# Attention in pieces between the units of a feed-forward layer

## The chip, the cores and the metric

The kernel runs on one core of one Trainium2 chip. The metric is the device time of one execution in microseconds, the median of several runs.

## The reference

Three stages follow one another. First attention over 4 batches, 8 heads, 576 positions and head size 64, with masks: heads 0 to 3 see the last 32 positions, heads 4 to 7 the earlier positions with the same remainder by 32.

```
scores = q @ k.T / 8, masked; attn = softmax(scores); x = attn @ v
x = x as (2304 tokens, 512)
h = max(x @ w1_in, 0);  x = (h * h) @ w1_out            # 512 -> 2048 -> 512
h = x @ w2_in
g = (a0 + a1 h + a2 h^2 + a3 h^3) / (1 + |b0||h| + |b1|h^2 + 1e-6)
out = g @ w2_out                                        # 512 -> 2048 -> 512
```

The weights come as 64-bit floats, the rest as 32-bit.

## The kernel before

The 2304 tokens are cut into six blocks of 384 (j = 0 to 5), the 2048 inner features into 16 slices of 128 (f = 0 to 15). Layer 1 runs all (j, f) in order, then layer 2 does. One step (j, f) of layer 1 is an h unit (`h_unit`, L412: 12 matmuls over four slices of the input, with each operand split into a high and a low part, three products), its activation (`act1`), and the output unit of the step two before (`o_unit1`, L452: 12 matmuls into four accumulators). Layer 2 has the same shape (L412, L605).

Attention is cut into 48 groups of two heads of one batch: a local group covers 192 queries, a strided one 14 or (every third pair of the strided) 4 of the 32 remainders. Groups are loaded and scored in pairs. A group goes through these functions: `at_scores` (a pair at a time, two PSUM banks; L277 puts the mask in by a matmul for groups before 24, L294 adds it on VectorE after that; L285 is q times k), `at_max` (L296, L297), `at_exp` (L309, four exponentials on ScalarE from the scores' bank), `at_norm` (L317, L318, and L320, where GpSimd multiplies e by the reciprocal), `at_transpose` (L327 on TensorE into a bank, L333 or L335 copies it to `at`), `at_values` (L343, a bank), and `at_out` (L368 on ScalarE and L369 on VectorE split the result into the high and low part of the layer's input). `last[j]` is the last group that block j needs: 9, 19, 23, 33, 43, 47.

The order is that of "slots" (`at_slot`). Slot n loads up to group n + 4, scores a pair if n is even, does the maximum of group n, the values of an earlier group, the transposes of one or two, the exponentials and the norm of n. The lags are three slots to the transposes and four to the values for groups before 12, two and three after that. Slots 0 to 13 run before layer 1 begins; the rest are put ahead of the h units by the table `ends`, always two slots at a time:

```
while slot < min(want, goal) or slot % 2 and slot < ends[-1]:
    at_slot(slot)
    slot += 1
```

By this two slots stand before units (0,0), (0,3), (0,6), (0,10), (0,13), (1,2), (1,6), (1,10), (2,0), (2,3), (2,7), (2,11), (3,0), (3,3), (3,6), (3,10), (3,13) and (4,3), a last one before (4,11).

PSUM has a pool of seven banks (tag "ps") for scores, transposes, values, h and accumulators, and one more bank (`psum_w`). An even block's four accumulators are all in the pool; an odd block's first one lies in the bank aside:

```
acc[j] = [acc_bank(f"acc0_{j}_{e}", e == 0 and j % 2 == 1) for e in range(KT)]
```

Weights of layer 1 are loaded raw (L189), turned into 32-bit floats with bit operations (`to_f32`: L201 on ScalarE, L202 to L204 on VectorE) and split (`split_w`: L218, L220, L221). The first four of 32 pieces are done in slots 10 to 13, the rest in block 0, two a step. In block 0 the low parts of the activation (L430) are VectorE's too. In blocks 1 to 4 the weights of layer 2 are converted in the same way and stored in memory (`spill_w`), eight pieces a block. Three blocks of the layer's input can live at a time.

All loads and stores are issued from SP's queue, in its order. q and k of a pair are one load (L250), its values another (L253); past group 12 each has two buffers. At the start SP issues q and k of the first pair, the masks, the first values, the identity, the coefficients `a` and `b` (L476, L477, broadcast to all partitions), and then q, k and values of three further pairs. ScalarE's first instruction is the absolute value of `b` (L478).

The program gives instructions in this order; a planner then orders each engine's queue by that order and by its own estimate of when operands and buffers are ready, except where `keep_in_program_order` or `issue_after` bind it (groups before 12 on TensorE, and layer 2). On the chip each engine follows its queue in order and waits where the real time comes later.

Of the kernel before, what the change touches and what calls it, by code (L numbers as in the profile page):

```python
# [9 lines left out]
F32 = mybir.dt.float32  # L10
# [3 lines left out]
AF = mybir.ActivationFunctionType  # L14
# [4 lines left out]
P = 128  # L19
B, H, S, D = 4, 8, 576, 64  # L20
# [5 lines left out]
NB = NT // TB  # L26
NF = DFF // P
# [98 lines left out]
QK_W = 1008  # L126
# [30 lines left out]
def moe_kernel(ctx, tc, qk, vp, w1, w2, a, b, masks, eye, out):  # L157
    nc = tc.nc
    groups = _groups()
    last = _last_group(groups)  # L160
    NG = len(groups)
# [70 lines left out]
    st = {}  # L232
    loaded = [0]
    FIRST, PLACES, LATE, WARM = 12, 8, 24, 10

    def lags(n):

        return (3, 4) if n < FIRST else (2, 3)

    def at_load(n):  # L240

        g, p = groups[n], n // 2
        if n < FIRST:
            t = wpool.tile([P, QK_W], F32, tag=f"wh{NF - 1 - p}", name=f"qk{g.name}")
            vt = wpool.tile([P, 2, 2, 2, D], F32, tag=f"w{'hl'[p % 2]}{7 - p // 2}", name=f"v{g.name}")
        else:
            t = apool.tile([P, QK_W], F32, tag="qk", name=f"qk{g.name}")
            vt = apool.tile([P, 2, 2, 2, D], F32, tag="v", name=f"v{g.name}")
        w = 2 * (g.qn + g.kn)
        nc.sync.dma_start(t[:, :w], qk[p][:, :w])  # L250
        if n == 0:
            nc.sync.dma_start(cst, masks)
        nc.sync.dma_start(vt, vp[p].rearrange("p (m t h d) -> p m t h d", m=2, h=2, d=D))  # L253
        for m in range(2):
            st[n + m] = dict(qk=t[m * D : (m + 1) * D], v=vt[:, m])

    def at_scores(n):

# [55 lines left out]
    def at_norm(n):  # L314
        g, s = groups[n], st[n]
        sm, nn = s["sm"], s["nn"]
        nc.gpsimd.tensor_scalar(sm[: g.nq, 8 : 8 + nn], sm[: g.nq, 8 : 8 + nn], 1.0, 1e-9, ALU.mult, ALU.add)  # L317
        nc.vector.reciprocal(sm[: g.nq, 12 : 12 + nn], sm[: g.nq, 8 : 8 + nn])  # L318
        r = sm[: g.nq, 12 : 12 + nn, None].to_broadcast([g.nq, nn, g.nk])
        nc.gpsimd.tensor_tensor(s["e"], s["e"], r, ALU.mult)  # L320
# [50 lines left out]
    def pin(n, ins):  # L371
        if n < FIRST:
            tc.keep_in_program_order(ins)

    def load_groups(n):
        while loaded[0] < min(NG, n):
            at_load(loaded[0])
            loaded[0] += 2

    def at_slot(n):  # L380

        load_groups(n + 4)
        if n < NG and n % 2 == 0:
            at_scores(n)
        if n < NG:
            at_max(n)
        if n == 2:
            warm_up(2)
        for m in range(max(0, n - 4), min(n, NG)):
            if n - m == lags(m)[1]:  # L390
                at_values(m)
        for m in range(max(0, n - 4), min(n, NG)):
            if n - m == lags(m)[0]:
                at_transpose(m)
        if n < NG:
            at_exp(n)
        for m in range(max(0, n - 4), min(n, NG)):
            if n - m == lags(m)[1]:
                at_out(m)
        if n < NG:  # L400
            at_norm(n)


    gt, acc, lows = {}, {}, []
# [66 lines left out]
            tc.keep_in_program_order(nc.tensor.matmul(wps, warm[:, :P], warm, start=True, stop=True))  # L471

    warm_up(6)
    load_groups(1)
    nc.sync.dma_start(ident, eye)
    nc.sync.dma_start(co[:, 0:4], a[None, :].to_broadcast([P, 4]))  # L476
    nc.sync.dma_start(co[:, 4:6], b[None, :].to_broadcast([P, 2]))  # L477
    nc.scalar.activation(co[:, 6:8], co[:, 4:6], AF.Abs)  # L478


    LAG, LATER = 2, 3
# [22 lines left out]
    def feed_w(n):  # L504
        for _ in range(n):
            load_raw(fed[0])
            if fed[0] < len(wq):
                f, part = wq[fed[0]]
                c = slice(part * DM, (part + 1) * DM)
                wh, wl = wt[0, f] if part else w_place(0, f)  # L510
                split_w(wh[:, c], wl[:, c], to_f32(0, f, part, raws[fed[0]]))
                fed[0] += 1

    load_groups(8)
    slot = 0
    while slot < last[0] + lags(0)[1] + 1:
        at_slot(slot)
        slot += 1
        load_raw(fed[0])
        if slot > 9:  # L520
            feed_w(1)
    steps = [(j, f) for j in range(NB) for f in range(NF)]
    prev = []

    attn_open = True
    n2 = 0

    def spill_w(f, part):
# [98 lines left out]

    prev2 = []
    LAG2, EARLY = 6, 5
    ends = [slot, 23, 30, 38, 47, 51]  # L630
    spills = (0, 8, 16, 24, 2 * NF)
    for j, f in steps:
        if attn_open:
            goal, start_slot = ends[j + 1], ends[j]
            want = start_slot + -(-(goal - start_slot) * (f + 1) // (NF - 1))
            while slot < min(want, goal) or slot % 2 and slot < ends[-1]:
                at_slot(slot)
                slot += 1
            if slot >= ends[-1]:
                attn_open = False  # L640
        while lows:
            lows.pop()()
        if j == 0:
            feed_w(2)
        ps = psum.tile([P, 512], F32, tag="ps", name=f"h0_{j}_{f}")
        h_unit(0, j, f, ps)
        last_act = act1(j, f, ps)
        if 0 < j < 5 and n2 < spills[j - 1] + -(-(spills[j] - spills[j - 1]) * (f + 1) // NF):
            with tc.issue_after(last_act):
                spill_w(n2 // 2, n2 % 2)  # L650
            n2 += 1
            if n2 == 2 * NF:
# [39 lines left out]
```

## Time and profile before

| what | value |
|---|---|
| time, median of 3 runs (lowest to highest) | 936.13 us (935.17 to 940.32) |
| the profiled execution's own time | 937.38 us |
| its span, first to last instruction | 935.6 us |
| TensorE matmul busy | 900.8 us, 96% |
| VectorE busy | 675.2 us, 72% |
| GpSimd busy | 595.5 us, 64% |
| ScalarE busy | 550.7 us, 59% |
| mean granted TensorE clock | 0.982 |
| first h unit; first h unit of block 5 | 47.84 us; 457.10 us |

Busy times are shares of the whole span, in which the stages have different limits: the time before the first h unit, block 0 with the weights' conversion, blocks 1 to 4 with attention, block 5, and layer 2. Matmuls overlap in the pipeline, so a run of twelve is read from start to start and not as twelve durations. A granted clock of 1.00 is 2.4 GHz, 0.50 is 1.2 GHz, and a figure between the two is the mean over a stretch that had both.

### The profile page before, as it was taken

The page shows a single profiled execution, that of the slowest core. Times are in us where ns is not written, and L with a number is a line of the kernel's source. Part 1 is how long each engine was busy: PE and PEld are TensorE (multiplying, and loading weights), DVE is VectorE, ACT ScalarE, POOL GpSimd, SP SyncE. Part 2 cuts the span into 40 slices and gives each one's busy share as a digit, 9 for nine tenths or more (in the row PEclk, how much of TensorE's full clock was granted, in tenths as well). Part 3 has the DMA queues.
Part 4 walks back from the last instruction along what each step waited for, and adds up shares of the span by engine and source line. Part 5 has one row for each costly group of instructions (what it writes and reads, how often), then busy time and mean ns, then how long its engine had stood idle before and what let it go on. Part 6 is the DMA issues. An engine that isn't in the chain of part 4 may idle for free.

```text
span 935.6 us, 14609 instructions
## 1 busy us (share of the span) xinstructions
PE 900.8 (96%) x5232; PEld 828.8 (89%) x5232; DVE 675.2 (72%) x792; ACT 550.7 (59%) x1391; POOL 595.5 (64%) x643
## 2 busy tenths in 40 slices
PE   6799989999989999999999999999999999999998
PEld 3598789998889898999999999999999899899896
DVE  3897965546444455434412589999999999999997
ACT  5786654445443544433324767777777776777774
POOL 3576755555444445534423478888888888888885
PEclk9799989999999999999999999999999999999999
DMA  8773334435433533433267530010010010100000
GB/s 294 258 268 120 121 111 167 165 112 192 151 121 98 170 101 130 145 124 113 95 234 262 194 133 9 9 50 9 9 51 9 18 43 9 43 1 1 34 1 34
DMA packets 40104, 98.55 MB, mean 105 GB/s; under 512 B 4704, under 2 KB 11616, under 8 KB 40032
## 3 DMA queue, kind: packets, MB, share of 16 engines
q1 hardware_dynamic: 40032, 97.62, 31.2%
q8 instruction: 41, 0.67, 0.3%
q14 instruction: 31, 0.25, 0.1%
HBM read 71.39 MB, written 26.21 MB: 104 GB/s over the span
## 4 chain that ended last, share of the span: by engine, by line
DVE 42%; PE 39%; ACT 2%; POOL 2%; issue 1%; DMA 1%; SPq 0%; POOLq 0%; ACTq 0%
DVE rq L572 23%; PE h L412 19%; PE acc L452 16%; DVE p L574 9%; DVE rq L583 7%; PE ps_t L327 1%; PE ps_v L343 1%; POOL spl L221 1%; PE ps_s L285 1%; DMA x_scratch<-x 1%; DVE r L426 1%; PE acc L605 1%; ACT w L201 1%; DVE w L202 0%; DVE w L203 0%
## 5 line engine op out<-in xcount | busy, mean ns | idle before, releaser
L412 PE MATMUL h<-xh,wh 128*128 128x384 f32 x768 | 260.3, 339 | 2.0 <-ACT at L335 0.9
L412 PE MATMUL h<-xh,wl 128*128 128x384 f32 x768 | 258.9, 337 | 0.0
L412 PE MATMUL h<-xl,wh 128*128 128x384 f32 x768 | 258.6, 337 | 0.0
L572 DVE RECIPROCAL rq<-w 128x384 f32<-128x384 f32 x96 | 243.9, 2541 | 17.2 <-POOL w L570 17.2
L412 PEld LDWEIGHTS h<-xh,wh 128*128 128x128 f32 x768 | 145.4, 189 | 8.7 <-ACT p L569 2.0
L412 PEld LDWEIGHTS h<-xl,wh 128*128 128x128 f32 x768 | 145.3, 189 | 3.8
L412 PEld LDWEIGHTS h<-xh,wl 128*128 128x128 f32 x768 | 145.2, 189 | 0.0
L430 POOL TENSOR_TENSOR gl<-r,gh 128x384 fp32r<-128x384 f32 x75 | 75.8, 1011 | 108.3 <-ACT gh L429 90.9
L591 POOL TENSOR_TENSOR gl<-rq,gh 128x384 fp32r<-128x384 f32 x96 | 115.1, 1199 | 39.8 <-ACT gh L590 39.8
L452 PE MATMUL acc<-gh,wh 128*128 128x384 f32 x384 | 132.2, 344 | 0.0
L452 PE MATMUL acc<-gh,wl 128*128 128x384 f32 x384 | 130.9, 341 | 0.8 <-POOL wl L221 0.8
L426 DVE TENSOR_TENSOR r<-r 128x384 f32<-128x384 f32 x75 | 54.4, 726 | 107.0 <-ACT r L422 106.9
L452 PE MATMUL acc<-gl,wh 128*128 128x384 f32 x384 | 131.3, 342 | 0.0
L570 POOL TENSOR_TENSOR w<-w,sq 128x384 f32<-128x384 f32 x96 | 97.5, 1015 | 46.5 <-ACT sq L567 46.3
L571 POOL TENSOR_TENSOR p<-p,hs 128x384 f32<-128x384 f32 x96 | 114.7, 1194 | 0.0
L605 PE MATMUL acc<-wh,gl 128*128 128x512 f32 x288 | 114.1, 396 | 0.3 <-POOL gl L591 0.3
L605 PE MATMUL acc<-wl,gh 128*128 128x512 f32 x288 | 113.7, 395 | 0.0
L605 PE MATMUL acc<-wh,gh 128*128 128x512 f32 x288 | 112.0, 389 | 0.0
L590 ACT CAST gh<-rq 128x384 fp32r<-128x384 f32 x96 | 49.4, 514 | 106.1 <-DVE rq L583 106.1
L422 ACT ACTIVATE r<-h 128x384 f32<-128x384 f32 x91 | 44.7, 491 | 98.7 <-PE h L412 94.5
L574 DVE SCALAR_TENSOR_TENSOR p<-p,co,hs 128x384 f32<-128x384 f32 x96 | 99.2, 1033 | 0.0
L429 ACT CAST gh<-r 128x384 fp32r<-128x384 f32 x91 | 46.8, 514 | 71.5 <-DVE r L426 71.1
(76 smaller groups left out, 1577.2 us busy)
## 6 DMA issues: line engine op xcount, KB each, us to landing
wraw<-in_w SPq DMA_DIRECT2D x64, 512.0 KB, 4.3
w_scratch<-sph SPq DMA_DIRECT2D x32, 256.0 KB, 4.0
w_scratch<-spl SPq DMA_DIRECT2D x32, 256.0 KB, 3.1
wh<-w_scratch SPq DMA_DIRECT2D x16, 512.0 KB, 3.7
wl<-w_scratch SPq DMA_DIRECT2D x16, 512.0 KB, 4.5
v<-in_vp SPq DMA_DIRECT2D x24, 256.0 KB, 4.7
qk<-in_qk SPq DMA_DIRECT2D x12, 416.0 KB, 4.6
x_scratch<-x SPq DMA_DIRECT2D x24, 192.0 KB, 3.1
```

The costliest lines, as they stand in the source:

```text
L412: nc.tensor.matmul(ps[:, :TB], w[:, c], x[:, kk, :], start=(kk == 0 and i == 0), stop=(kk == KT - 1 and i == 2))
L426: nc.vector.tensor_tensor(h, h, h, ALU.mult)
L430: low = lambda: (nc.vector if psum_h or j == 0 else nc.gpsimd).tensor_tensor(gl, h, gh.bitcast(F32), ALU.subtract)
L452: nc.tensor.matmul(acc[j][e][:, :TB], w[:, c], g, start=(f == 0 and i == 0), stop=(f == NF - 1 and i == 2))
L570: keep(nc.gpsimd.tensor_tensor(w, w, sq, ALU.add))
L571: keep(nc.gpsimd.tensor_tensor(p1, p1, hs, ALU.mult))
L572: keep(nc.vector.reciprocal(rq, w))
L574: keep(nc.vector.scalar_tensor_tensor(p1, p1, a1, hs, ALU.add, ALU.mult))
L583: keep(nc.vector.scalar_tensor_tensor(rq, p1, a0, rq, ALU.add, ALU.mult))
L590: keep(nc.scalar.copy(gh, rq))
L591: keep(nc.gpsimd.tensor_tensor(gl, rq, gh.bitcast(F32), ALU.subtract))
L605: nc.tensor.matmul(p, g[:, t * P : (t + 1) * P], w[:, c], start=(f == 0 and i == 0), stop=(f == NF - 1 and i == 2))
```

## The change

Slots stay for groups up to slot 13. Past them attention is a list of pieces, and at most one stands before a unit. A piece is either the values of group v with the transposes of group v + 1, or a pair's scores with maximum, exponentials and norms of both groups. Two of the first kind come, then one of the second. `paces` spreads the 55 pieces over blocks 0 to 4 as 14, 10, 13, 13 and 5. q and k of the pair after next are loaded after a pair's scores, values of the pair after next after the pair's second values; both from pair 8 on. At the start Exp is ScalarE's first instruction, q and k of the second pair are loaded ahead of the first values, and the coefficients are loaded (and their absolute value taken) before unit (3,0).

```diff
+    def load_qk(p):            # q and k of pair p; load_v(p) likewise its values
...
     def load_groups(n):
-        while loaded[0] < min(NG, n):
-            at_load(loaded[0])
+        while loaded[0] < min(2 * AHEAD_PAIRS, n):      # AHEAD_PAIRS = 8
+            load_qk(loaded[0] // 2)
+            load_v(loaded[0] // 2)
             loaded[0] += 2
+    def pieces(n):
+        t, v = n - 3, n - 4
+        yield from ()
+        while v < NG:
+            for _ in range(2):
+                yield v, t
+                v, t = v + 1, t + 1
+            if n < NG:
+                yield n
+                n += 2
+
+    def at_piece(piece):
+        nonlocal slot
+        if isinstance(piece, int):
+            at_scores(piece)
+            for n in (piece, piece + 1):
+                at_max(n)
+                at_exp(n)
+                at_norm(n)
+            load_qk(piece // 2 + 2)
+            return
+        v, t = piece
+        if v < NG:
+            at_values(v)
+            slot = max(slot, v + 5)
+        if t < NG:
+            at_transpose(t)
+        if v < NG:
+            at_out(v)
+            if v % 2 and v // 2 + 2 >= AHEAD_PAIRS:
+                load_v(v // 2 + 2)
...
     warm_up(6)
-    load_groups(1)
+    nc.scalar.activation(co[:, 9:10], co[:, 8:9], AF.Exp)
+    load_qk(0)
+    nc.sync.dma_start(cst, masks)
+    load_qk(1)
+    load_v(0)
     nc.sync.dma_start(ident, eye)
-    nc.sync.dma_start(co[:, 0:4], a[None, :].to_broadcast([P, 4]))
-    nc.sync.dma_start(co[:, 4:6], b[None, :].to_broadcast([P, 2]))
-    nc.scalar.activation(co[:, 6:8], co[:, 4:6], AF.Abs)
+    load_v(1)
+    loaded[0] = 4
+    def load_co():             # the three lines above, as they were
...
-    ends = [slot, 23, 30, 38, 47, 51]
+    load_qk(AHEAD_PAIRS)
+    todo = list(pieces(slot))
+    due_by = [next(i for i, p in enumerate(todo) if isinstance(p, tuple) and p[0] == last[j]) + 1 for j in range(1, NB)]
+    paces = [due_by[0], max(due_by[1], due_by[0] + 10), max(due_by[2], due_by[0] + 23), due_by[3], len(todo)]
+    done = [0]
     for j, f in steps:
-        if attn_open:
-            goal, start_slot = ends[j + 1], ends[j]
-            want = start_slot + -(-(goal - start_slot) * (f + 1) // (NF - 1))
-            while slot < min(want, goal) or slot % 2 and slot < ends[-1]:
-                at_slot(slot)
-                slot += 1
+        if j < NB - 1:
+            start = paces[j - 1] if j else 0
+            want = start + -(-(paces[j] - start) * (f + 1) // NF)
+            while done[0] < want:
+                at_piece(todo[done[0]])
+                done[0] += 1
...
+        if (j, f) == (3, 0):
+            load_co()
```

## Rows read from the trace of the kernel before

**Rows 1.** The page: busy tenths of TensorE and its granted clock, 40 slices.

```profile
PE   6799989999989999999999999999999999999998
...
PEclk9799989999999999999999999999999999999999
```

**Rows 2.** Stretches from block to block: length, each engine's busy us (instructions), clock, DMA.

```profile
47.84:136.34 88.50, 81.42 (x512) 74.87 (x511) 73.49 (x132) 59.69 (x171) 62.96 (x76) 0.94 0.44 150
136.34:217.31 80.97, 80.97 (x556) 77.29 (x556) 43.24 (x72) 38.93 (x117) 41.52 (x52) 1.00 0.49 159
217.31:307.49 90.18, 84.49 (x537) 79.06 (x537) 42.64 (x81) 39.96 (x130) 41.99 (x56) 0.96 0.41 133
307.49:386.46 78.97, 76.59 (x504) 72.06 (x504) 40.77 (x82) 38.20 (x124) 40.79 (x55) 0.98 0.41 129
386.46:457.10 70.64, 69.60 (x418) 68.11 (x418) 30.98 (x46) 24.24 (x49) 31.38 (x31) 1.00 0.35 115
457.10:519.50 62.40, 62.40 (x362) 62.40 (x362) 13.48 (x19) 23.12 (x48) 20.84 (x22) 1.00 0.65 228
```

**Rows 3.** The same stretches, TensorE's instructions of L452 alone, blocks 0 to 4.

```profile
47.84:136.34 88.50, 36.77 (x168) 0.94 0.44 150
136.34:217.31 80.97, 40.18 (x203) 1.00 0.49 159
217.31:307.49 90.18, 41.55 (x205) 0.96 0.41 133
307.49:386.46 78.97, 34.68 (x171) 0.98 0.41 129
386.46:457.10 70.64, 36.35 (x193) 1.00 0.35 115
```

**Rows 4.** Block 0, TensorE's instructions of L277 alone (mask matmuls).

```profile
47.84:136.34 88.50, 2.08 (x8) 0.94 0.44 150
```

**Rows 5.** Waits of TensorE, 47.8 to 457 us: us in total, times, longest.

```profile
PE ps_t L327 <- ACT e L309: 5.8, 5, 1.7
PE ps_t L327 <- DVE xl L369: 5.1, 3, 2.5
PE ps_v L343 <- ACT at L335: 3.3, 4, 1.0
```

**Rows 6.** Timeline of one burst in block 2: start, us, what [idle before].

```profile
228.15 0.48 PE L285 MATMUL ps_s<-qk 64*72 64x72 f32 x8
...
231.98 0.32 ACT L309 ACTIVATE e<-ps_s,sm 72x72 f32<-72x72 f32 x1 [2.33 <-POOL sm L297]
...
232.06 0.30 DVE L294 TENSOR_TENSOR ps_s<-ps_s,cst 72x144 f32<-72x144 f32 x1
...
232.74 0.65 PE L327 MATMUL ps_t<-ident,e 126*126 126x126 f32 x4 [1.73 <-ACT e L309]
...
235.21 0.30 ACT L309 ACTIVATE e<-ps_s,sm 72x72 f32<-72x72 f32 x1
```

**Rows 7.** VectorE's groups in block 0: count | busy us, mean ns | idle before.

```profile
L204 DVE SCALAR_TENSOR_TENSOR wraw<-wraw,bits 128x512 int32<-128x512 int32 x28 | 19.1, 683 | 0.7
...
L296 DVE TENSOR_REDUCE sm<-ps_s 96x4 f32<-96x512 f32 (+1 forms) x8 | 4.6, 581 | 0.0
```

**Rows 8.** Stretches before the first h unit, columns as in rows 2.

```profile
41.20:47.84 6.64, 6.20 (x58) 4.78 (x56) 5.96 (x13) 6.17 (x29) 3.22 (x8) 0.74 0.69 222
20.50:47.84 27.34, 20.55 (x193) 15.01 (x189) 24.66 (x55) 21.67 (x100) 14.59 (x30) 0.81 0.80 274
```

**Rows 9.** Timeline of the start.

```profile
3.06 0.43 SPq L477 DMA_DIRECT2D co<-in_b  x1
...
7.72 0.20 POOL L297 TENSOR_SCALAR sm<-sm 126x4 f32<-126x4 f32 x1 [7.28 <-DVE sm L296]
...
9.55 0.20 ACT L478 ACTIVATE co<-co 128x2 f32<-128x2 f32 x1 [7.54 <-DMA co<-in_b]
...
10.81 1.67 PE L285 MATMUL ps_s<-qk 64*126 64x126 f32 x16 [3.32 <-DMA qk<-in_qk]
```

More of the change, by code (lines that the diff above doesn't have):

```diff
@@ L238, in lags, with load_v @@
         return (3, 4) if n < FIRST else (2, 3)
-    def at_load(n):
-        g, p = groups[n], n // 2
+    def load_qk(p):
+        n = 2 * p
+        if n >= NG:
+            return
+        g = groups[n]
         if n < FIRST:
             t = wpool.tile([P, QK_W], F32, tag=f"wh{NF - 1 - p}", name=f"qk{g.name}")
+        else:
+            t = apool.tile([P, QK_W], F32, tag="qk", name=f"qk{g.name}")
+        w = 2 * (g.qn + g.kn)
+        nc.sync.dma_start(t[:, :w], qk[p][:, :w])
+        for m in range(2):
+            st[n + m] = dict(qk=t[m * D : (m + 1) * D])
+    def load_v(p):
+        n = 2 * p
+        if n >= NG:
+            return
+        g = groups[n]
+        if n < FIRST:
             vt = wpool.tile([P, 2, 2, 2, D], F32, tag=f"w{'hl'[p % 2]}{7 - p // 2}", name=f"v{g.name}")
         else:
-            t = apool.tile([P, QK_W], F32, tag="qk", name=f"qk{g.name}")
             vt = apool.tile([P, 2, 2, 2, D], F32, tag="v", name=f"v{g.name}")
[L249 to L252, printed above, removed]
         nc.sync.dma_start(vt, vp[p].rearrange("p (m t h d) -> p m t h d", m=2, h=2, d=D))
         for m in range(2):
-            st[n + m] = dict(qk=t[m * D : (m + 1) * D], v=vt[:, m])
+            st[n + m]["v"] = vt[:, m]
     def at_scores(n):
@@ L373, in pin @@
             tc.keep_in_program_order(ins)
+    AHEAD_PAIRS = 8
     def load_groups(n):
-        while loaded[0] < min(NG, n):
-            at_load(loaded[0])
+        while loaded[0] < min(2 * AHEAD_PAIRS, n):
+            load_qk(loaded[0] // 2)
+            load_v(loaded[0] // 2)
             loaded[0] += 2
@@ L382, in at_slot @@
         load_groups(n + 4)
-        if n < NG and n % 2 == 0:
+        if n % 2 == 0:
             at_scores(n)
-        if n < NG:
-            at_max(n)
+        at_max(n)
         if n == 2:
             warm_up(2)
-        for m in range(max(0, n - 4), min(n, NG)):
+        for m in range(max(0, n - 4), n):
             if n - m == lags(m)[1]:
                 at_values(m)
-        for m in range(max(0, n - 4), min(n, NG)):
+        for m in range(max(0, n - 4), n):
             if n - m == lags(m)[0]:
                 at_transpose(m)
-        if n < NG:
-            at_exp(n)
-        for m in range(max(0, n - 4), min(n, NG)):
+        at_exp(n)
+        for m in range(max(0, n - 4), n):
             if n - m == lags(m)[1]:
                 at_out(m)
-        if n < NG:
-            at_norm(n)
+        at_norm(n)
[14 more added lines that the diff above has]
+            for n in (piece, piece + 1):
+                at_max(n)
+                at_exp(n)
+                at_norm(n)
+            load_qk(piece // 2 + 2)
+            return
+        v, t = piece
[8 more added lines that the diff above has]
+                load_v(v // 2 + 2)
     gt, acc, lows = {}, {}, []
@@ L473, in moe_kernel @@
     warm_up(6)
-    load_groups(1)
-    nc.sync.dma_start(ident, eye)
-    nc.sync.dma_start(co[:, 0:4], a[None, :].to_broadcast([P, 4]))
-    nc.sync.dma_start(co[:, 4:6], b[None, :].to_broadcast([P, 2]))
-    nc.scalar.activation(co[:, 6:8], co[:, 4:6], AF.Abs)
+    nc.scalar.activation(co[:, 9:10], co[:, 8:9], AF.Exp)
[3 more added lines that the diff above has]
+    load_v(0)
+    nc.sync.dma_start(ident, eye)
+    load_v(1)
+    loaded[0] = 4
+    def load_co():
+        nc.sync.dma_start(co[:, 0:4], a[None, :].to_broadcast([P, 4]))
+        nc.sync.dma_start(co[:, 4:6], b[None, :].to_broadcast([P, 2]))
+        nc.scalar.activation(co[:, 6:8], co[:, 4:6], AF.Abs)
     LAG, LATER = 2, 3
@@ L515, in moe_kernel @@
     slot = 0
-    while slot < last[0] + lags(0)[1] + 1:
+    while slot < last[0] + 5:
         at_slot(slot)
@@ L523, in moe_kernel @@
     prev = []
-    attn_open = True
     n2 = 0
@@ L629, in moe_kernel @@
     LAG2, EARLY = 6, 5
-    ends = [slot, 23, 30, 38, 47, 51]
+    load_qk(AHEAD_PAIRS)
[3 more added lines that the diff above has]
+    done = [0]
     spills = (0, 8, 16, 24, 2 * NF)
     for j, f in steps:
-        if attn_open:
-            goal, start_slot = ends[j + 1], ends[j]
-            want = start_slot + -(-(goal - start_slot) * (f + 1) // (NF - 1))
-            while slot < min(want, goal) or slot % 2 and slot < ends[-1]:
-                at_slot(slot)
-                slot += 1
-            if slot >= ends[-1]:
-                attn_open = False
+        if j < NB - 1:
[4 more added lines that the diff above has]
+                done[0] += 1
         while lows:
```

## The prediction

> **What bounds the kernel now.** I began with the page: TensorE is busy for 900.8 of 935.6 us and its row of the 40 slices holds 9 nearly everywhere after slice 18; the lower digits, and all the lower digits of the granted clock, lie in the first 18 slices [rows 1]. So the time is TensorE's stream, and what can move lies in the start and in the five blocks of layer 1 that carry attention. The second view cuts these into blocks, from one block's first h unit to the next's [rows 2]. Block 5 has no attention: 16 h units and 14 output units, 360 matmuls in 62.40 us, 0.1733 us each, 2.08 a unit of 12, at clock 1.00. With that price and the count of output matmuls (the x of [rows 3], less one that reaches over the edge except in the first row; h is 192 each time, by the code) each block splits into layer work and the rest:
> block 0: 360 matmuls 62.4, rest 26.1; block 1: 394, 68.3, rest 12.7; block 2: 396, 68.6, rest 21.5; block 3: 362, 62.7, rest 16.2; block 4: 384, 66.6, rest 4.1.
> Block 1 carries four pairs of groups with no idle time (80.97 busy of 80.97) at clock 1.00, so 12.7/4 = 3.17 us is what a pair costs when nothing is late, the breaks of the stream included. Blocks 0, 2 and 3 carry four pairs of which one has groups with half the heads' tiles, 28/32 of block 1's: 11.1, and block 0 has 2.1 of mask matmuls on top (8 of them, for groups before number 24 [rows 4]). Block 4 has a quarter: 3.2. Lost are then 12.9, 0, 10.5, 5.1 and 0.9, together 29.4 us; 7.1 + 5.7 + 2.4 + 1.0 = 16.2 of it is idle (stretch less PE busy in [rows 2]) and 13.2 is the low clock around it (0.94, 0.96 and 0.98 as means of these blocks).
> What TensorE waits for is in the next view [rows 5]. A transpose reads e, which GpSimd wrote last (L320), so one that waits for ScalarE at L309 (the exponential) or VectorE at L369 does not wait for data: it waits for a PSUM bank that a pair of scores or another group's values still hold. These are 10.9 of the 16.2 us; 3.3 are values that wait for the copy of their own transposes. The blocks say why: an even block gives all four accumulators banks of the pool of seven, an odd block puts one aside, so three and four banks are left. The even blocks 0, 2 and 4 idle 13.8 us, the odd ones 2.4. One burst shows it [rows 6]: scores at 228.15, eight matmuls; the next transpose comes 1.73 us late at 232.74, as the exponentials that free the banks run at 231.98 and at 235.21 for the second group, behind mask additions on VectorE at 232.06.
>
> **The change part by part.** The step is priced on the profiled execution: 937.38 us, of which 935.6 is the span; the median of the runs shown is 936.13, 1.25 lower.
> *Pieces.* From group 14 on the same instructions run, only elsewhere: nothing is taken from TensorE's 328.6 us of layer matmuls or from the clean price. What goes is two slots in one unit, which ask for two score banks, two value banks, two transpose banks and one for h, with three or four free. Now a unit gets values plus transposes (two banks and h's) or a pair's scores (two and h's): three fit. Values come a piece after their transposes, a unit of 4.16 us later, so the 3.3 us for the copy should go. Transposes come two pieces after their scores, over 8 us; in the burst shown the first group's bank was free 4.4 us after its scores, the second's about 7.4 [rows 6], so the second can still be late by up to about 2. Next late is then h: with scores held it has one bank, freed by a Relu that stands behind exponentials in ScalarE's order.
> Blocks 2 to 4: 16.5 us can go, none has to. I take two thirds, 11.0, as the first bank is in time by those rows and the second not always. Block 1 loses nothing now and gives nothing.
> Block 0 has a second limit. VectorE converts weights there: 28 of the third step at 0.683 us [rows 7], 2.05 a piece with its three steps. From 41.20 (the scores of pair 14) to 136.34 it is busy 5.96 + 73.49 = 79.5 of 95.1 us [rows 2, 8]. One pair moves to block 1 and takes about 2.1 of it along (two reductions of 0.6 [rows 7], their reciprocals, one group's values), leaving 77.4. TensorE needs 62.4, 4.8 pairs' worth of attention at 3.17 and 2.1 of masks: 79.7. Two engines of nearly the same load that feed one another don't reach either floor: in the 27 us before, VectorE reached 24.66 of 27.34, 90% [rows 8], and 77.4/0.90 is 86. So 95.1 falls to 86, less 2.7 for the pair's work that block 1 now does: 6.4 gained. Bounds: 12.7 if TensorE's own 79.7 decides, 0 if VectorE's order is as late as now.
> The number of breaks stays near three a pair, so they cost nothing over 3.17; an upper end of 2 us for all 17 pairs, as an estimate, is kept in the range.
> *Start.* ScalarE's first instruction waits 7.54 us for the coefficients' load, to 9.55, while GpSimd had the first exponential's bias at 7.92 [rows 9]: 1.6 us go when Exp comes first and the coefficients leave. Two loads leave SP's queue ahead of the second pair's q and k, and the first v goes behind them, so these are issued at about 1.65 instead of 3.54; TensorE waits 3.32 us for them [rows 9]. Everything behind moves with ScalarE's exponentials, but weights and VectorE take over from 20 us on (24.66 of 27.34). I take 1.5, near the 1.6 of the row; ends 0 and 3.3.
> *Coefficients in block 3.* Two small loads and an Abs, on an engine that runs in order: Relu stands behind it. At the start that load took 6.5 us from issue [rows 9]; the planner may put the Abs too early, with four banks left in block 3 as cover of about a unit. I take 0.5; ends 0 and 6.5. The page "DMA: Bandwidth & Descriptors" of the Trainium skill (Latency and other measured facts) puts a small transfer's fixed cost near 2 us and says that it shrinks with lighter load on memory; by it the unit hides the load and the term is 0, and the sum 0.5 lower. No row of this kernel shows that load in a quiet stretch.
> *Loads of q, k and v* follow the piece that frees their buffers, five or more pieces before their use, over 20 us against landings of under 5: nothing of TensorE's waits past the start names them [rows 5], so 0 either way. Behind a blocked one on SP's queue stand weight loads; the new order blocks it less.
> Sum: -1.5 - 6.4 - 11.0 + 0.5 = -18.4; 937.4 - 18.4 = 919.0, and 1.25 lower on the median's footing: 918.
>
> **The rivals.**
> *Everything goes*: the start gives 3.3, block 0 comes down to TensorE's floor, no bank is late: -3.3 - 12.7 - 16.5 = -32.5, 904 on the median's footing. For it: block 1 has no idle at all. Against it: VectorE's load in block 0.
> *VectorE holds block 0*: -1.5 - 11.0 + 0.5 = -12.0, 924. For it: 79.5 of 95.1; against it: VectorE itself idles 15.0 of 88.5 us in that block [rows 2], when TensorE stalls.
> *The pieces do not do what they say*: the bank is late by its exponential's latency and not by the crowd, so only the 3.3 us for copies and a part of the start go: about 4, 932. For it: the bias came late in the burst shown because VectorE had other work in front; against it: odd blocks hold the same latencies and idle 2.4.
> *Slower*: each pair's scores keep two of the three banks for up to 7.4 us, longer than the unit they now stand in front of, h is left with one bank, and every one of the 17 pairs pays what a pair of block 2 loses now, 10.5/4 = 2.6 us with the clock's fall: 44.6 in place of 29.4 + 2.4 (the stretch before the first unit lost 2.4, 6.64 [rows 8] less about 4.2 of clean work, 1.3 pairs' worth). That is +12.8, with the start 947. It decides above 31.8/17 = 1.9 us a pair. Against it: block 1 has the same order on ScalarE and pays 0. The page "TensorE: Matmul & The Clock Gate" of the Trainium skill (A second HAM failure mode: psum-queue depth-cycling) speaks for it: a kernel that cycled through PSUM banks idled briefly so often that its clock kept falling back. By that rule more, smaller pieces would be dear even with free banks; this trace bears it out only where TensorE did idle, block 1 is broken as often and keeps clock 1.00.
>
> **How the numbers follow.** What a measurement of this kernel can tell from no change is about 0.5%, 4.7 us. Forecast 918 (its own range 912 to 923): 0.50. Everything goes, 904: 0.10. VectorE holds block 0, 924: 0.21. Pieces without effect, 932: 0.11, within 0.5%. Slower, 947: 0.08. So faster 0.81, same 0.11, slower 0.08. The range 907 to 932 leaves out the slower case, half of 904 and half of 932.
>
> **What would show it.** Right: blocks 2 and 4 idle under 2 us each at clock 1.00; no wait of values for L335's copy; the first exponential near 8 us; block 0, from the first piece, near 86 us with VectorE at 90%. Wrong: transposes or h units that still wait for L309 or L369 in even blocks; ScalarE idle in block 3 for the coefficients; block 0 as long as now per piece. In block 5 and in layer 2 nothing should change.

## The result and the profile after

| | before | after |
|---|---|---|
| median | 937.98 us (11 runs, 931.97 to 943.28) | 929.12 us (11 runs, 927.95 to 930.35) |
| profiled execution, its span | 937.38, 935.6 | 929.01, 927.2 |
| mean granted clock | 0.982 | 0.987 |
| first h unit of blocks 0, 1, 5 | 47.84, 136.34, 457.10 | 42.25, 136.06, 448.10 |

The ratio is 0.991 (95%: 0.9885 to 0.9936): faster by 0.6 to 1.2%. That is 8.9 us between the medians, where 18 were forecast, and 8.4 between the profiled executions. Line numbers moved: the h unit is now L457, the output unit L497, scores L296, transposes L338, values L354, the exponential L320, GpSimd's scaling of the maximum L308.

The page's slices answer to [rows 1]:

```profile
PE   7799889999999999999999999999999999999998
...
PEclk9799899999999999999999999999999999999999
```

The low digits are now all in the first six slices, some 139 us; from there on TensorE and its clock hold 9, up to the last slice. The table by block says the same in numbers and answers to [rows 2] (from one block's first h unit to the next's: us; busy us and count of TensorE, its weight loads, VectorE, ScalarE, GpSimd; clock, DMA share, GB/s):

```profile
42.25:136.06 93.81, 85.33 (x541) 78.07 (x539) 74.88 (x135) 59.96 (x168) 62.62 (x74) 0.94 0.43 142
136.06:214.50 78.44, 77.60 (x519) 73.71 (x517) 41.17 (x71) 36.73 (x120) 42.67 (x53) 1.00 0.45 148
214.50:296.60 82.10, 80.67 (x540) 75.00 (x538) 43.98 (x83) 39.33 (x127) 43.24 (x56) 1.00 0.47 148
296.60:377.75 81.15, 80.43 (x544) 75.11 (x542) 41.20 (x81) 38.11 (x124) 41.36 (x55) 1.00 0.47 149
377.75:448.10 70.35, 70.35 (x430) 68.88 (x429) 33.98 (x52) 27.50 (x67) 33.31 (x36) 1.00 0.33 110
448.10:510.50 62.40, 62.40 (x361) 62.40 (x361) 13.75 (x19) 23.13 (x48) 21.12 (x22) 1.00 0.66 229
```

Blocks 1 to 4 take 312.04 us against 320.76. They idle (length less the first busy figure) 0.84 + 1.43 + 0.72 + 0 = 2.99 us where they idled 9.1 by [rows 2], and the clock is 1.00 in all four. What TensorE waits for from 136.06 to 448.10 is short (us in total, times, longest; answers to [rows 5]):

```profile
PE ps_t L338 <- ACT e L320: 1.8, 4, 0.8
PE h L457 <- ACT e L320: 0.7, 2, 0.4
PE ps_v L354 <- ACT e L320: 0.5, 1, 0.5
```

VectorE's split (xl) and the copy of the transposes have gone from the list. Block 0 is the other story. It begins 5.6 us earlier, because some attention moved from before it into it, and ends where it did. The h matmuls alone, before, in two stretches (length; us of TensorE busy and count, the same of its weight loads; clock, DMA share, GB/s):

```profile
41.20:83.00 41.80, 13.34 (x72) 12.46 (x72) 0.92 0.66 226
83.00:136.34 53.34, 22.54 (x121) 21.66 (x122) 0.94 0.31 100
```

and after:

```profile
41.20:83.00 41.80, 21.70 (x108) 19.44 (x108) 0.96 0.60 200
83.00:136.06 53.06, 19.59 (x87) 17.71 (x85) 0.90 0.31 100
```

At 83 us the new kernel is nine units on (108 matmuls, 12 a unit) where the old one was six. It then gives all three back by 136.

The whole account of the 8.4 us: the first piece starts 0.4 earlier (40.80 against 41.20), of which 0.3 is left at block 1 (136.06 against 136.34); blocks 1 to 4 give 8.7; block 5 is 62.40 in both; what follows it, layer 2 to the end, is 0.6 longer (from block 5's start to the end 479.1 against 478.5). 0.3 + 8.7 - 0.6 = 8.4.

What TensorE waits for in block 0 after the change:

```profile
PE ps_v L354 <- ACT e L320: 2.6, 2, 1.8
PE h L457 <- ACT r L467: 2.3, 2, 1.9
PE acc L497 <- POOL wl L221: 2.2, 2, 1.5
```

They name ScalarE and the split weights, none of them VectorE directly. TensorE idles 93.81 - 85.33 = 8.5 us there. What ScalarE itself waits for in that block:

```profile
ACT e L320 <- POOL sm L308: 7.9, 4, 4.0
ACT w L201 <- DMA wraw<-in_w: 7.4, 3, 3.3
```

Its timeline shows one such wait and what stands behind it (start, us, instruction, idle before):

```profile
85.83 2.31 ACT L201 ACTIVATE w<-wraw 128x512 f32<-128x512 f32 x4 [2.91 <-DMA wraw<-in_w]
88.05 0.47 ACT L467 ACTIVATE r<-h 128x384 f32<-128x384 f32 x1
...
94.24 0.36 ACT L320 ACTIVATE e<-ps_s,sm 96x128 f32<-96x128 f32 x1 [3.96 <-POOL sm L308]
```

ScalarE stands until 85.83 for the raw weights of one piece. Four conversions (x4) run then, and only after them the Relu of an h unit, at 88.05, for which TensorE waits:

```profile
88.67 0.66 PE L457 MATMUL h<-xh,wh 128*128 128x384 f32 x1 [1.89 <-ACT r L467]
```

The other engines stand with it. VectorE, which takes the converted piece next:

```profile
86.53 0.69 DVE L202 TENSOR_SCALAR bits<-w 128x512 int32<-128x512 int32 x1 [3.25 <-ACT w L201]
...
91.84 0.68 DVE L307 TENSOR_REDUCE sm<-ps_s 96x4 f32<-96x512 f32 x1
```

and GpSimd, which splits it:

```profile
80.42 1.31 POOL L221 TENSOR_TENSOR wl<-wraw,wh 128x512 fp32r<-128x512 f32 x1 [0.93 <-ACT wh L218]
...
88.84 0.67 POOL L220 TENSOR_SCALAR wh<-wraw 128x512 fp32r<-128x512 f32 x1 [4.50 <-DVE wraw L204]
...
92.74 1.31 POOL L221 TENSOR_TENSOR wl<-wraw,wh 128x512 fp32r<-128x512 f32 x1
94.01 0.34 POOL L308 TENSOR_SCALAR sm<-sm 96x4 f32<-96x4 f32 x2
```

So the stall comes back a second time. A pair's scores (L296, from 85.66 for 1.12 us) were there at 86.78, but VectorE reaches the maximum only at 91.84, behind the conversions that it began 3.25 us late, and has it ready at 91.84 + 0.68 = 92.52. The splits, 4.50 us late, are in GpSimd's queue ahead of the small scaling of that maximum; the scaling runs at 94.01, the exponential at 94.24, and TensorE waits again:

```profile
96.35 0.35 PE L354 MATMUL ps_v<-at,v 72*64 72x72 f32 x4 [1.76 <-ACT e L320]
```

Behind both stalls the granted clock falls to 0.50, which is 1.2 GHz (columns as in [rows 2]):

```profile
88.60:91.90 3.30, 3.23 (x10) 3.26 (x11) 3.16 (x6) 1.64 (x3) 1.98 (x2) 0.50 0.18 73
98.90:105.60 6.70, 6.32 (x21) 6.20 (x22) 4.04 (x9) 1.76 (x7) 5.77 (x7) 0.50 0.26 81
```

The matmuls of the unit at 88.67 start 0.32 us apart, those of the unit before it 0.17. Half of these 10 us, some 5 as an estimate from these rows, come on top of the 8.5 that TensorE idles.

The load was late because of its place, the low half of weight slice 12, which an earlier raw piece had used. GpSimd finished with that piece at 80.42 + 1.31 = 81.73. SP issued four loads one after the other, this piece's last, behind those of three later pieces. The row ends at 82.09, so this load was issued as its place came free, and it landed some 4 us later:

```profile
73.83 8.26 SPq L189 DMA_DIRECT2D wraw<-in_w  x4
```

### The profile page after: what moved, and what is told of

Same layout as the page of the kernel before. It is cut to its first block, busy times and chain, and to the rows that moved or that the text cites. A ratio compares the mean times of both kernels' runs of the same rounds, so it can differ in the third digit from the quotient of the medians.

```text
span 927.2 us, 14645 instructions
## 1 busy us (share of the span) xinstructions
PE 899.6 (97%) x5232; PEld 825.7 (89%) x5232; DVE 674.2 (73%) x792; ACT 548.1 (59%) x1392; POOL 599.1 (65%) x643
## 4 chain that ended last, share of the span: by engine, by line
DVE 44%; PE 43%; POOL 4%; ACT 4%; DMA 3%; issue 2%; POOLq 0%; SPq 0%; DVEq 0%; ACTq 0%
DVE rq L624 24%; PE h L457 20%; PE acc L497 17%; DVE p L626 9%; DVE rq L635 7%; PE ps_s L296 2%; PE ps_v L354 2%; POOL wl L221 2%; PE ps_t L338 2%; ACT e L320 1%; DVE wraw L204 1%; DMA qk<-in_qk 1%; DMA wraw<-in_w 1%; DVE bits L203 1%; ACT w L201 1%
## 5 line engine op out<-in xcount | busy, mean ns | idle before, releaser
L457 PE MATMUL h<-xh,wh 128*128 128x384 f32 x768 | 264.8, 345 | 3.8 <-ACT r L467 2.3
L457 PE MATMUL h<-xh,wl 128*128 128x384 f32 x768 | 259.6, 338 | 0.0
L457 PE MATMUL h<-xl,wh 128*128 128x384 f32 x768 | 259.1, 337 | 0.0
L457 PEld LDWEIGHTS h<-xh,wh 128*128 128x128 f32 x768 | 145.8, 190 | 12.0 <-issue 2.6
L457 PEld LDWEIGHTS h<-xl,wh 128*128 128x128 f32 x768 | 145.8, 190 | 3.8
L457 PEld LDWEIGHTS h<-xh,wl 128*128 128x128 f32 x768 | 145.4, 189 | 0.0
L497 PE MATMUL acc<-gh,wl 128*128 128x384 f32 x384 | 129.5, 337 | 2.2 <-POOL wl L221 2.2
L497 PE MATMUL acc<-gh,wh 128*128 128x384 f32 x384 | 129.3, 337 | 1.3 <-ACT wh L218 0.9
L497 PE MATMUL acc<-gl,wh 128*128 128x384 f32 x384 | 128.5, 335 | 0.0
L471 DVE TENSOR_TENSOR r<-r 128x384 f32<-128x384 f32 x75 | 51.7, 689 | 81.9 <-ACT r L467 81.5
```

What stands on the lines that cost most here:

```text
L457: nc.tensor.matmul(ps[:, :TB], w[:, c], x[:, kk, :], start=(kk == 0 and i == 0), stop=(kk == KT - 1 and i == 2))
L471: nc.vector.tensor_tensor(h, h, h, ALU.mult)
L497: nc.tensor.matmul(acc[j][e][:, :TB], w[:, c], g, start=(f == 0 and i == 0), stop=(f == NF - 1 and i == 2))
```

## The experiments

"Block 0" is from its first h unit to block 1's, a profiled execution each; times are medians with their lowest and highest, ratios against the kernel before on the same chip. The edits are shown shortened. A profile is of one execution: in e4, e7, e9, e10 and e11 it is the fastest one, and in e1 and e3 it lies 4.1 and 2.4 us under the median.

**e1, the new start alone, on the kernel before.**

```diff
+    nc.scalar.activation(co[:, 9:10], co[:, 8:9], AF.Exp)
+    load_qk(0); masks; load_qk(2); load_v(0); ident; load_v(2)
+        if (j, f) == (3, 0):
+            load_co()
```

> The kernel before with the changed start alone (Exp first, second pair's q and k ahead of the first values, coefficients loaded before unit (3,0)), slots in pairs as before. In the changed kernel the first piece began only 0.4 us sooner than the first slot of block 0 did, and block 0 ended at the same time. If the pieces made the whole gain: first h unit of block 5 at 456 to 457 us against 457.1, time 0 to 1.5 us under before. If the start carries a share that block 0 hides in the changed kernel: block 5 at 452 to 454.

936.50 us (931.25 to 941.61), ratio 0.9969 (0.9944 to 0.9994): some 3 us, small but there. Block 0 runs from 46.79 to 133.79, 87.0 us.

**e2, the pieces alone, with the old start.**

```diff
-    load_qk(0); masks; load_qk(1); load_v(0); ident; load_v(1); Exp first
+    load_qk(0); masks; load_v(0); ident; co from a, b; Abs
```

> The changed kernel with the old start (coefficients first, Abs as ScalarE's first instruction). If the pieces made the whole gain: 8 to 9 us under before, block 5 at 448 to 449. If the start is needed: 4 to 6 us under before, block 5 at 451 to 453.

927.22 us (926.78 to 927.54), ratio 0.9873 (0.9855 to 0.9891). So the pieces alone give all of the gain and, by the medians, a little more than the whole change; of the start's share nothing is left when both are there. Block 0 is 43.70 to 136.52, again ending at 136.5; blocks 1 to 4 are 310.7. ScalarE waits 12.2 us for raw weights in block 0, more than the 7.4 of the whole change, in a block that is 1 us shorter.

**e3, the kernel before with the spare bank given to the even blocks 2 and 4.**

```diff
-            acc[j] = [acc_bank(f"acc0_{j}_{e}", e == 0 and j % 2 == 1) for e in range(KT)]
+            acc[j] = [acc_bank(f"acc0_{j}_{e}", e == 0 and j % 2 == 0 and j > 0) for e in range(KT)]
```

> The kernel before with the bank aside given to the even blocks 2 and 4 instead of 1, 3 and 5: three free banks in blocks 1 and 3, four in 2 and 4. If crowded banks made the idle time: block 2 loses under 3 us instead of 10.5, block 4 nothing, block 1 loses 6 to 12 instead of 0, block 3 stays at 5 or above. If the latency of scores, maximum and exponentials made it: block 1 stays at 0 idle and block 2 keeps 4 to 6 us idle.

934.80 us (931.74 to 938.23), ratio 0.9951 (0.9935 to 0.9968). Blocks 1 to 4:

```profile
135.43:219.78 84.35, 83.41 (x568) 79.39 (x567) 44.52 (x73) 39.54 (x124) 42.77 (x53) 1.00 0.48 154
219.78:299.84 80.06, 77.11 (x514) 72.44 (x514) 40.25 (x79) 36.93 (x116) 40.37 (x53) 1.00 0.45 148
299.84:381.74 81.90, 77.70 (x515) 72.38 (x515) 40.38 (x83) 39.11 (x130) 41.43 (x56) 1.00 0.38 125
381.74:452.26 70.52, 69.31 (x418) 68.14 (x418) 30.88 (x47) 24.93 (x50) 31.96 (x31) 1.00 0.35 116
```

Block 2, given the bank, idles 2.95 us in place of 5.7; block 3, which lost it, 4.20 in place of 2.4; but block 1, which lost it too, idles only 0.94, and block 4, which got it, 1.21 in place of 1.0. The transposes' own waits go with the bank: 0.9 us in block 2 where they were 4.6, 3.7 in block 3 where they were 1.4. In e1, with the old bursts and banks, the idle times of these blocks are within 0.1 of those before, so the differences are the edit's. But together the four blocks idle 9.3 us, as before 9.1: the idle time moved. That they take 316.8 us in place of 320.8 is the clock, 1.00 in all, and e1, where it was 0.99 with the old banks, took 318.0. So the number of banks matters and does not decide alone. Why block 1 gets by with fewer stays open.

**e4, the whole change with less work on VectorE in block 0.** The step that puts the weights' signs in is left out in layer 1, so the weights there have no signs.

```diff
-        nc.vector.scalar_tensor_tensor(bits, hi, -0x80000000, bits, ALU.bitwise_and, ALU.bitwise_or)
+        if layer:
+            nc.vector.scalar_tensor_tensor(bits, hi, -0x80000000, bits, ALU.bitwise_and, ALU.bitwise_or)
```

> The changed kernel without the second VectorE step (the sign bit, 0.69 us) in the conversion of layer 1's weights; the weights' signs are left out. VectorE has 19 us less to do in block 0. If VectorE's load holds block 0: its 93.8 us from first h unit to first h unit fall to 80 to 86, and the time by 8 to 13. If late raw weights hold it (raw loads that wait for a split to free their place, 4 us from issue to use): it stays at 90 or above, with ScalarE still waiting for raw loads 6 us or more.

929.40 us (928.87 to 930.16), ratio 0.9899 (0.9878 to 0.9921). Block 0:

```profile
43.30:137.89 94.59, 85.39 (x540) 77.87 (x539) 57.37 (x103) 58.15 (x164) 63.40 (x75) 0.94 0.44 148
```

VectorE is busy for 57.37 us where it was 74.88, and the block is no shorter: less load on VectorE alone does not help it (for the limits of this test see e12).

**e5, the whole change with three raw pieces in the staging buffers, not in weight places that an earlier piece has to leave.**

```diff
+    for k in (17, 19, 21):
+        homes[k] = (None, 0)
```

> The changed kernel with three raw weight loads of layer 1 (pieces 17, 19 and 21 of 32) put into stage buffers that are idle in block 0, instead of places that an earlier piece's split frees just before. Theory 'late raw loads': ScalarE, which runs in order, stands still for a late load at 82.9 to 85.8 us and Relu and exponentials stand behind it; then block 0 falls from 93.8 to 86 to 90 us, ScalarE's wait for raw loads there from 7.4 to under 4, and the time by 4 to 8. Rival 'GpSimd's queue' (the two tiny operations of a group's softmax stand behind splits of 0.7 and 1.3 us): block 0 within 2 us of 93.8.

922.46 us (921.64 to 923.44), ratio 0.9821 (0.9806 to 0.9836).

```profile
42.43:132.59 90.16, 83.72 (x541) 77.10 (x539) 73.65 (x134) 60.60 (x167) 64.47 (x75) 0.95 0.45 147
```

Block 0 falls from 93.81 to 90.16 with no instruction taken away. The first stall is gone. Up to it TensorE and GpSimd run the same instructions in the same order as in the changed kernel; on ScalarE the conversions that stood four in a row behind the late load now run one by one from 76.26 on, without a wait for raw weights up to 100 us, and the Relu that ran at 88.05 runs at 84.69:

```profile
76.26 0.68 ACT L201 ACTIVATE w<-wraw 128x512 f32<-128x512 f32 x1 [0.30 <-DVE bits L202]
...
84.69 0.49 ACT L467 ACTIVATE r<-h 128x384 f32<-128x384 f32 x1
```

The 13th unit starts at 104.61 in place of 112.46. More than half of these 8 us are lost again before the block's end, and ScalarE's waits for raw weights in the block are still 6.7 us, where under 4 was expected. What is left shows the same pattern, a late load on ScalarE, an exponential behind it, and TensorE behind that:

```profile
110.22 1.21 ACT L201 ACTIVATE w<-wraw 128x512 f32<-128x512 f32 x2 [2.95 <-DMA wraw<-in_w]
...
111.33 0.35 ACT L320 ACTIVATE e<-ps_s,sm 96x128 f32<-96x128 f32 x1
```

```profile
112.86 0.55 PE L354 MATMUL ps_v<-at,v 128*64 128x96 f32 x8 [3.81 <-ACT e L320]
```

**e6, the whole change with the two tiny softmax steps (4 columns at most) on VectorE.**

```diff
-        nc.gpsimd.tensor_scalar(sm[: g.nq, 4 : 4 + nn], sm[: g.nq, 0:nn], -1.0 / 8.0, 0.0, ALU.mult, ALU.add)
+        nc.vector.tensor_scalar(sm[: g.nq, 4 : 4 + nn], sm[: g.nq, 0:nn], -1.0 / 8.0, 0.0, ALU.mult, ALU.add)
-        nc.gpsimd.tensor_scalar(sm[: g.nq, 8 : 8 + nn], sm[: g.nq, 8 : 8 + nn], 1.0, 1e-9, ALU.mult, ALU.add)
+        nc.vector.tensor_scalar(sm[: g.nq, 8 : 8 + nn], sm[: g.nq, 8 : 8 + nn], 1.0, 1e-9, ALU.mult, ALU.add)
```

> The changed kernel with the two tiny operations of each group's softmax (scaling of the maximum, adding 1e-9 to the sum) on VectorE instead of GpSimd. 'GpSimd's queue': waits for the scores' banks in block 0 go, it falls to 87 to 90 us, blocks 1 to 4 lose their last 3 us of idle time, 5 to 9 us in all. 'Late raw loads': block 0 stays within 2 us, 0 to 3 us in all from blocks 1 to 4.

926.29 us (922.80 to 927.36), ratio 0.9856 (0.9829 to 0.9883). Block 0 is 92.20, within 2 us of 93.81, as was expected if late raw loads hold it. The scaling no longer stands behind a split on GpSimd, as it did at 94.01 in the changed kernel.

**e7, e2 with e5's edit: the old start, raw places mended.**

```diff
+    for k in (17, 19, 21):       # on e2
+        homes[k] = (None, 0)
```

> The pieces with the old start (927.2 us as measured) and the three raw loads in idle stage buffers. 'Late raw loads': 920 to 924. 'GpSimd's queue': 926 to 928.

925.28 us (923.61 to 926.85), ratio 0.985 (0.9834 to 0.9866), between the two expectations. With the old start the edit is worth 1.9 us by the medians (927.22 in e2, on another chip, and the intervals overlap), with the new one 6.7 (929.12 to 922.46, from two series of runs): what the places cost depends on the order around them. Against e5 on the same chip: with the raw places mended the new start is worth 925.28 - 922.46 = 2.8 us, as alone in e1.

**e8, e5 and e6 together.**

```diff
+    for k in (17, 19, 21):
+        homes[k] = (None, 0)
-        nc.gpsimd.tensor_scalar(sm ...)      # both, as in e6
+        nc.vector.tensor_scalar(sm ...)
```

> The changed kernel with both edits, raw loads in idle buffers and the tiny operations on VectorE. If both delays hold block 0 in turn: 915 to 921, block 0 at 82 to 86. If only one counts: the better of the two alone, within 2 us.

921.64 us (919.81 to 922.95), ratio 0.981 (0.9794 to 0.9827). The runs overlap with e5's: beside e5, e6's edit adds nothing that these runs can tell, as was expected if only one of the two delays counts.

**e9, the whole change with raw pieces 16 to 27 laid out anew**: four in staging (the text below says three) and every other one in a place whose last piece is four or more back. Six of the twelve change their place, and piece 19 of e5's edit does not.

```diff
+    homes[16:28] = [(c, 0) for c in ("h12", None, "h13", "l13", "h14", None,
+                    "h15", "l14", "l15", None, "h15", None)]
```

> The changed kernel with raw pieces 16 to 27 of layer 1's weights put so that each buffer's last user is four or more pieces back (three of them in stage buffers). With pieces 17, 19 and 21 alone 922.5 us were measured, ScalarE still waited 6.7 us for raw loads and one wait of TensorE of 3.8 us stood behind one of them. 'Late raw loads': ScalarE's wait under 4 us, block 0 at 85 to 88, 917 to 921. If the rest of block 0 is the chain through GpSimd and VectorE: block 0 at 89 to 91, 921 to 924.

920.22 us (919.34 to 921.13), ratio 0.9805 (0.9757 to 0.9853).

```profile
41.23:128.72 87.49, 82.69 (x542) 75.83 (x540) 74.25 (x136) 60.99 (x173) 64.01 (x75) 0.96 0.47 154
```

Block 0 is 6.3 us shorter than in the changed kernel, yet ScalarE still waits 6.6 us there for raw weights, where under 4 was expected. So the total of these waits does not measure the harm; it is TensorE's idle time (85.33 of 93.81 busy, then 82.69 of 87.49: 8.5 us, then 4.8) that fell.

**e10, e9 and e6 together.**

```diff
+    homes[16:28] = [ ... ]                   # as in e9
-        nc.gpsimd.tensor_scalar(sm ...)      # both, as in e6
+        nc.vector.tensor_scalar(sm ...)
```

> The same with the two tiny softmax operations on VectorE. 'Late raw loads' with a second, smaller share of GpSimd's queue: 914 to 919, block 3 without idle time. If the tiny operations matter only where raw loads are late: within 1 us of the kernel without this edit.

918.52 us (915.24 to 920.90), ratio 0.9792 (0.9741 to 0.9843): the lowest median here. Its runs overlap with e9's (919.34 to 921.13), so that e6's edit adds anything beside e9's is not shown.

```profile
40.79:126.54 85.75, 82.40 (x541) 75.36 (x539) 79.30 (x153) 60.37 (x171) 59.84 (x58) 0.97 0.46 152
```

VectorE now does more than in the changed kernel (79.30 us against 74.88), in a block 8.1 us shorter, in the fastest of four executions. ScalarE waits 8.0 us there for raw weights, more than the 7.4 in the changed kernel.

**e11, the whole change with raw pieces loaded four ahead, not eight.**

```diff
-    AHEAD = 8
+    AHEAD = 4
```

> The changed kernel with raw loads at most 4 pieces ahead instead of 8: the opposite direction, later loads. 'Late raw loads': ScalarE waits longer for them than 7.4 us in block 0, which grows to 96 us or more, 931 to 938. 'GpSimd's queue' or a bound in VectorE's work: block 0 within 2 us of 93.8.

930.07 us (928.91 to 931.47), ratio 0.9908 (0.9876 to 0.9939): the changed kernel's time within the noise, where 931 to 938 was expected.

```profile
41.28:137.97 96.69, 86.29 (x542) 75.34 (x540) 79.20 (x139) 61.16 (x173) 62.91 (x76) 0.96 0.48 157
```

Block 0 grows by 2.9 us as expected, but not in the way expected: ScalarE waits less for raw weights (6.1 us), and TensorE waits for the split weights themselves:

```profile
PE acc L497 <- POOL wl L221: 3.9, 6, 1.4
PE acc L497 <- POOL wh L220: 2.4, 2, 2.0
```

**e12, e9 without the step for the signs** (weights of layer 1 without signs, as in e4), to see whether VectorE limits block 0 once the loads are in time.

```diff
+    homes[16:28] = [ ... ]                   # as in e9
+        if layer:                            # as in e4
```

> The kernel with raw pieces 16 to 27 placed anew (block 0 at 87.5 us, 920.2) without the sign step of layer 1's conversion on VectorE; the weights' signs are left out. If VectorE's load is what holds block 0 once the raw loads are in time (the floor of 86 that the prediction gave it): block 0 falls to 80 to 83 and the time to 913 to 916. If ScalarE's standing for raw loads and the scores' banks still hold it: block 0 stays within 2 us of 87.5.

929.63 us (929.18 to 930.86), ratio 0.988 (0.9857 to 0.9904), against both expectations.

```profile
43.81:139.23 95.42, 84.46 (x541) 77.10 (x539) 53.78 (x103) 58.01 (x164) 63.14 (x75) 0.94 0.43 147
```

With 20 us less work on VectorE block 0 is 7.9 us longer than in e9. ScalarE's timeline shows the long waits back (L321 and L309 are the exponential and the scaling here):

```profile
75.76 0.66 ACT L201 ACTIVATE w<-wraw 128x512 f32<-128x512 f32 x1 [4.68 <-DMA wraw<-in_w]
...
94.39 0.67 ACT L201 ACTIVATE w<-wraw 128x512 f32<-128x512 f32 x1 [5.49 <-DMA wraw<-in_w]
...
104.95 0.36 ACT L321 ACTIVATE e<-ps_s,sm 96x128 f32<-96x128 f32 x1 [5.34 <-POOL sm L309]
```

The planner orders each queue by its own estimates, and shorter work changes that order: ScalarE's and VectorE's queues differ from e9's from before 28 us on, long before these waits. That a queue laid out for loads that then come later stands is how the waits read; no run has the less work in e9's order. This limits e4 and e12 as tests: they took away work and changed the order too. VectorE's load as the limit falls all the same, since e10 has a shorter block with more of it.

## Why the prediction was off

Of the 10.0 us by which the profiled execution (929.0) missed the forecast of 919.0, block 0 makes 9.3 (from the first piece to block 1 it was to take 86 and took 95.3), the start 1.1 (the first piece was to come 1.5 earlier and came 0.4), block 5 to the end 0.6; blocks 1 to 4 with 0.4 and the coefficients with 0.5 were better than forecast.

**The start, 1.5: not seen in the sum.** The step put the first exponential near 8 us. It came at 9.20, against 9.66 before:

```profile
9.20 0.37 ACT L320 ACTIVATE ea<-ps_s,sm 126x126 f32<-126x126 f32 x1 [6.97 <-POOL sm L308]
```

ScalarE no longer waits for the coefficients, as forecast, but for the bias, which [rows 9] had at 7.72 + 0.20 and which now came 1.25 later. The scores ahead of it took longer, 2.07 us for 16 matmuls at 6.10, where they took 1.15 at 5.78 before:

```profile
6.10 2.07 PE L296 MATMUL ps_s<-qk 64*126 64x126 f32 x16
```

With the same start e5 and e9 show 1.15 again, and the first exponential at 7.68 and 7.91, near 8 as forecast; e1 and e10 show 2.07. This is TensorE's clock. The trace's list of granted clocks has its first entry, 1.00, at 10.07 us in the changed kernel, in e1 at 10.08 and in e10 at 8.67; before, and in e5 and e9, at 4.4 to 4.8. In all fourteen profiles the scores take 1.15 where that entry comes before 5 us and 2.07 where it comes after 8 (PEclk reads 1.00 where the list has no entry). The ratio 2.07 to 1.15 is near that of the unit at 88.67 at 1.2 GHz, 0.32 to 0.17. So the scores ran at the lower level here; why the clock rose later, with the same six warm-up matmuls ahead from 1.49 to 4.23 us, is open. The step had taken the row of the kernel before as it was, with the clock already high; in nine of the fourteen profiles it was not yet. The start itself is worth 3 us by e1 and 2.8 by e7 against e5, near the upper end of 3.3, but only where block 0 passes it on. In the changed kernel it did not.

**Block 0, 6.4: the step that failed.** The term took 95.1 us, from the first piece to block 1, down to 86, with VectorE at 90% as the only limit. It is 95.3 (40.80 to 136.06), although a pair, priced at 2.7, had left it: as long as before, which was named as a sign of being wrong. The bound of 0 was named for it ("if VectorE's order is as late as now"), and the rival for it put 0.21 on VectorE. That bound means 95.1 - 2.7 = 92.4, so the block came out 2.9 beyond even that, and the cause was not the rival's either: VectorE itself stood 3.25 us at 86.53 for ScalarE, e4 took 17.5 us from VectorE without effect, and e10 added 4.4 us and was shorter. What the step left out, as the traces read, is that an earlier run of units asks for their weights earlier. Nine units by 83 us in place of six leave each raw piece less time between the moment its place is free and the conversion that needs it; ScalarE waited 3.6 us for raw weights in block 0 before and 7.4 after. The forecast counted VectorE's work for weights, and neither the loads nor what stands behind a late one on ScalarE. That the loads' places cost time here is shown: other places for three of them give 3.7 us in block 0, six others in e9 6.3. For the first stall e5 shows the mechanism too: with the load in time the stall is gone, while TensorE and GpSimd keep their order. Beyond it the mechanism is read from single waits such as that at 110.22. ScalarE's waits for raw weights in sum do not follow the gain (7.4 in the changed kernel, 6.7, 6.6 and 8.0 in e5, e9 and e10, 12.2 in e2); since a new layout also lets the planner order ScalarE's and VectorE's queues anew, how much of the rest is the wait itself and how much the order stays open. In e10 the stretch from the first piece (39.34) to block 1 is 87.2 us, and VectorE is busy for 79.30 of the 85.75 from the first h unit, 92%: in the fastest execution of the fastest kernel the 86 and the 90% nearly come out, though ScalarE still waits for loads there. Whether VectorE is then the limit is not shown.

A page of the Trainium skill ("Perfetto Trace Analysis", Tensor Engine Instruction) states that ScalarE's queue, like VectorE's and GpSimd's, is strictly first in, first out, and only TensorE's reorders, for weight loads. The Relu at 88.05 behind a load that was late until 85.83 agrees; the page gives no price for it.

**Blocks 2 to 4, 11.0: right in size.** Blocks 1 to 4 fell by 8.7, and the forecast had 11.0 less the 2.7 for the pair that moved into block 1, 8.3. The signs asked for came out: block 4 idles 0, block 2 1.43 (under 2), both at 1.00; values no longer wait for the copy. The sign of being wrong came out in small: transposes and h units still wait for the exponential, the transposes 1.8 us (0.6 of it in block 2) where it was 3.4 in the same blocks, so the step that the second bank may still be late holds. The gain is the pieces': in every run with pieces blocks 1 to 4 take 309.4 to 312.0 us, in e1 and e3 with the old bursts 318.0 and 316.8. That it came from banks rather than from the order of the engines' queues is not settled: e3 gave the bank to other blocks, and the transposes' waits moved with it in blocks 2 and 3, but block 1 hardly changed and the idle time of all four stayed.

**Coefficients, 0.5: it cost nothing, and stood elsewhere.** The planner put the loads into block 0:

```profile
61.80 0.43 SPq L529 DMA_DIRECT2D co<-in_a  x1
...
66.20 0.42 SPq L530 DMA_DIRECT2D co<-in_b  x1
```

and the absolute value at 71.47, with no idle time of ScalarE ahead of it. That is 5.3 us behind the second issue. From issue to landing the two loads took 5.0 and 3.0 us by the trace's DMA view. The term 0, which followed from the Trainium skill's "DMA: Bandwidth & Descriptors" (Latency and other measured facts), is what happened; the trace agrees in that the load was quicker than at the start (6.5 us by [rows 9]), and differs in that both took longer than the page's fixed cost near 2 us.

**Rivals.** "Everything goes" needed block 0 at 79.7 and falls. "Slower" fell with blocks 1 to 4: a piece keeps the clock at 1.00 there. The rule weighed beside it (the Trainium skill, "TensorE: Matmul & The Clock Gate", A second HAM failure mode: psum-queue depth-cycling) did not come to bear: 41 pieces in blocks 1 to 4 over the same banks left TensorE idle for only 3.0 of 312 us, and there was no low clock. "Pieces without effect" put 932, 3 us above the median, but its cause fell by e2, which gains 1.1 to 1.5% by pieces alone.

## What to carry to other kernels

When a change makes one engine reach its work earlier, price the loads that feed that work, and ask what place each goes into and which instruction frees it; a load that is late stops everything behind its consumer on an engine that runs in order. A floor computed from busy times of two engines is worth having (e10's profile came to 87.2 against 86), but it is a forecast only if nothing else that the stage waits for comes late. Cutting work is no clean test where a planner orders the queues: an experiment that moves a buffer or an instruction says more when the timeline is read for the wait it removed.

## What was not expected

Removing work lengthened a stage: 20 us less on VectorE, and block 0 went from 87.49 to 95.42 (e9, e12). And the spread of the times changed: the kernel before ran from 931.97 to 943.28, e1 and e3 with the same bursts from 931.25 to 941.61 and from 931.74 to 938.23; the changed kernel from 927.95 to 930.35 and e2 from 926.78 to 927.54. That pieces steady the time in general is not shown: e6 and e10, which have them too, spread over 4.6 and 5.7 us in four runs.
